# Fused local and pooled attention with a gated MLP: a new stored order, and TensorE's mask and direct pooled product kept for four head pairs instead of six

## The chip, the cores and the metric

The kernel runs on one core of one Trainium2 chip. The metric is the device time of one execution in microseconds (us). Of the kernel before, three timed runs are shown; their median is 613.86 us (613.84 to 614.27).

## The reference

Eight batches, eight heads, 576 positions, head size 64. Attention is computed twice for each head and added: once on queries, keys and values averaged over groups of 4 positions (144 of them, the result repeated 4 times), once on all positions with a mask that leaves only |i - j| < 4. The sum goes through a spatially gated MLP.

```python
q_d, k_d, v_d = (t.reshape(B, H, Sd, 4, D).mean(axis=3) for t in (q, k, v))
out_up = np.repeat(sm_attn(q_d, k_d, v_d), 4, axis=2)
scores = np.where(np.abs(pos[:, None] - pos[None, :]) < 4, scale * q @ k.T, -1e9)
x = (out_up + softmax(scores) @ v)             # heads joined: (8, 576, 512)
h = gelu_tanh(x @ w_in);  u, v = h[..., :512], h[..., 512:]
v_s = einsum('ts,bsd->btd', w_sg, layernorm(v) * g_ln) + b_sg
out = x + (u * v_s) @ w_out
```

The large products need more than one TensorE pass: each operand is split into a high and a low half, and high x high, high x low and low x high are accumulated.

## The kernel before, in words

The work is written as tasks. A task has a name, the engines it may run on and a function that emits its instructions. The string `ORDER` lists all tasks with the engine of each (`ks2/P` is task ks of pair 2 on POOL); `place` (line 60) reads it and hands out the buffers, and the loop at the end emits the tasks in that order. Each engine therefore works through its own tasks in the order of the string, and waits where an input is not there yet. Costs of tasks stand in the `add` calls, but nothing in the built program depends on them. Eight PSUM banks (`ps`), ten buffers `X` and forty buffers `R` are shared by everything. In the rows, a number behind a buffer's name is that of the tile which uses it.

There are 32 head pairs (g = 0 to 31, two heads of 64 rows beside each other), four to a batch, and one MLP block to a batch. For a pair, TensorE does:

- `S` (scores, line 408): the local scores in ten windows, 64x64 tiles, 40 instructions of line 420.
- `Y` (scores_d, 436): the pooled scores, 64x144 tiles, 12 instructions of line 442.
- `T`, `U`, `t` (turn, turn2, turn3, lines 509 to 525): transpositions of the weights of attention, 128x128 and 72x128 tiles, lines 512, 517 and 522. All three together are called turns below.
- `d` (av_d, 544): the pooled product with the values, line 552, 72x64 tiles.
- `D` (av, 565): the local product with the values, 64x58 tiles, 40 instructions of line 573.

S, Y and D contract over 64 rows; they are called 64-row work below. The MLP products are the wide work: `v` and `vk` (line 665, 128x512) and `u`, `s`, `o` (line 743, 128x288), called from `v_mm`, `u_mm`, `s_mm`, `o_mm`.

Pairs 0 to 5 are early (`early = g < EARLY`, line 365). In an early pair TensorE itself adds the mask: `scores` first writes the mask into the two banks by a product with the identity (line 413, 4 instructions), and `top` (line 451) and `exp` read the banks. In later pairs VectorE (DVE) adds the mask in two steps, `ma` and `mb` (line 428), which also free the banks, and `top` is one reduction (453). In an early pair `d` multiplies the values of all four positions of a group (32 instructions); in later pairs GpSimd (POOL) first sums them (`vs`, lines 404 and 405, four instructions) and `d` has 8 instructions.

While the first pairs run, the weights are prepared: 24 pieces of 64-bit input words are turned into a high and a low half by shift, flush, total, high and low (lines 296 to 324) on DVE, ScalarE (ACT) and POOL, and w_sg by lines near 351. The first block's `u0.x`, `s0.x` and `o0.x` need them. `gl0.3` (line 799) is the last DVE step ahead of the first output product `o0.6`.

Of the kernel before, what the change touches and what calls it, by code (L numbers as in the profile page):

```python
# [89 lines left out]
wty3/P ks4/P S3 qs4/V wby6 mx3 wqy4 wqy6 wfy4 wfy6 t1 T1 wuz5 U1 wuy6 pa1/A re2/A pb1/A d0 wby1 rc2 nx3/A Y3 why2/V  # L90
np2/V pc1/A wqy1 wty4/P why4/V wfy1 wbz4 my3 wly7/V ea3 od0 wty6/P lw2 wuz7 pe1/A T2 pa2/A nq2/P D0 wly0/P xa0
wly5/P wqz4 U2 t2 wfz4 wur2 ny3/A why6/A wuz4 ec3 wuz6 wty1/P pb2/V wly4/P d1 wbz5 pc2/V xb0 why1/V wqz5 eb3 xh0/V
why3/V wbz7 pe2/V wfz5 wly1/P wly6/P od1 wuz1 wr3 lv2 S4 wz3 lw3 lw4 wq0 wqz7 mx4 re3/A wuz0 wur1 qs5/P nx4/A ea4
eb4 lv3 lq6 wr5 wq4 wr7 lk6 wq1 xl0/P Y4 D1 my4 d2 rc3 xa1 wfz7 xb1 nq3/V wly2/V xh1/V ny4/V ec4 lv4 np3/P wbz6 wbz0
wr0 wqz6 od2 xl1/P wly3/P wqz0 re4/A S5 vk2.0 T3 wtz7/P xc1 mx5 wfz0 rc4 wfz6 vk1.0 vk2.1 D2 lw5 lq7 pa3/A t3 U3
np4/V xa2 whz7/V xb2 nx5/A ea5 vk1.1 wuz2 eb5 pb3/V pc3/V xh2/V pe3/A wtz5/P wur5 whz5/A whq3/A nq4/P vk0.0 t4 T4 U4
pa4/A wlz7/V ks5/V wtz0/P wbz1 qs6/V pb4/V whz0/A wqz1 pc4/A wuz3 d3 wbz2 wfz1 wtz4/P wtz6/P xl2/P vk0.1 wlz0/P xc2
xc0 od3 wqz2 pe4/A wbz3 whz6/A wqz3 vk1.2 wfz2 D3 xa3 wfz3 xb3 wtz1/P whz1/A xh3/A vk2.2 Y5 my5 ny5/A d4 ks6/P
wlz1/P xl3/P wbr1 ec5 wbr3 re5/V qs7/V lk7 wtz3/P wqr1 od4 wqr3 wur3 wfr1 rc5 xc3 wtz2/P wlz5/V np5/P wbr5 wfr3
# [5 lines left out]
u0.3 ua0.3 vl0.2/V Y6 T5 wbr2 wur4 wqr2 wfr7 my6 whr1/A xc4 pa5/V s0.0 sa0.0 ks8/P wtr7/P sm0.0/P wlr5/P wlr1/P ec7
ny6/A s0.1 U5 pb5/A lq8 qs8/V wbr0 wbr6 sa0.1 wqr0 ec6 whr7/V wfr2 wqr6 s0.2 sa0.2 wfr0 wtr2/V wlr7/V wfr6 pc5/V
sm0.1/P nx6/A eb6 gh0.0/A s0.3 s0.4 t5 s0.5 lv5 sm0.2/P wtr6/P sa0.3 wbr4 wtr0/P s0.6 sm0.3/P ea6 sa0.4 wqr4 re6/A
whr2/A gh0.1/A whr0/A wfr4 gl0.0/V whr6/A sa0.5 rc6 sm0.5/V sm0.4/V gl0.1/V sa0.6 pe5/A s0.7 nq6/V sa0.7 np6/V
sm0.7/V wlr2/P sm0.6/P wtr4/P wlr0/V whr4/V d5 Y8 U6 gh0.2/A my8 lw6 od5 lv6 gh0.3/A gl0.2/P D5 lw7 gl0.3/V T6 xa5
# [5 lines left out]
vg1.0 vg1.2 vb1.0 vp1.0 vb1.2 vp1.2 nq9/P va1.4/V vj1.4 T9 d8 od8 v1.1 vn1.0 pa9/V vn1.2 vg1.1 vg1.3 lv9 U9 D8 t9
vb1.1 xa8 pb9/V S10 ma10 u1.3 u1.1 u1.0 vh1.0/A ua1.2 ua1.3 vg1.4 vp1.1 vn1.1 xb8 vh1.1/A xh8/A vb1.3 lq12 os0.3
os0.1 lk11 mb10 pc9/V vp1.3 mx10 vn1.3 vh1.3/A pe9/A u1.4 Y10 ua1.0 lk12 vh1.2/A ua1.4 nx10/A ua1.1 vs9 d9 lw10
os0.2 u1.6 lv10 vb1.4 vp1.4 vl1.3/V vn1.4 od9 D9 lw11 my10 vh1.4/A vl1.1/V vl1.0/P xl8/P u1.7 ks11/P vs10 xa9 S11
vl1.4/V vl1.2/V qs12/V xb9 u1.5 ea10 ny10/A eb10 ec10 s1.4 s1.0 ma11 re10/V rc10 nq10/V xc8 np10/P ks12/P lk13 lq13
# [840 lines left out]
```

## Time and profile before

| | |
|---|---|
| median of 3 runs | 613.86 us |
| the profiled execution | 612.97 us |
| its span, first to last instruction | 611.2 us (1.8 us lie around it) |
| granted TensorE clock, mean | 0.997 |
| first TensorE instruction | 6.1 us after the span's start |
| TensorE instructions | 6600 |
| DMA | 58.10 MB, mean 95 GB/s |

The profile is of one execution. A timeline row has the start in us, the time from the first start to the last end of its instructions, the engine, the line, the operation, what it writes and reads, the tiles' shapes and the count; behind it, in brackets, the idle time ahead of it and what ended it. TensorE's instructions overlap, so what a step costs its successors is read from one start to the next start, not from the length in its row. A windows row has a stretch of the span, its length, and for PE, PEld, DVE, ACT and POOL the busy time with the number of instructions, then the granted clock, the mean busy share of the DMA engines and GB/s.

### The profile page before, as it was taken

To read this page: it belongs to the slowest core of one execution; us is meant where nothing else is said; L and a number is where in the kernel's file an instruction comes from. 1 tells how busy PE (TensorE), PEld (TensorE's weight loads), DVE (VectorE), ACT (ScalarE), POOL (GpSimd) and SP (SyncE) were. 2 spreads that over 40 slices of the span, in tenths; PEclk is the share of its full clock that TensorE was granted. 3 is DMA by queue.
4 is the path that set the end of the run, shared out by engine and by line. 5 is a ranking of instruction groups with operands and counts; after the bars stand their busy time and mean duration, and the time that the engine had idled before them with its cause. 6 is when DMAs were issued, how large, how long until landed. Compare 5 with 4: busy or idle time off the path is not lost.

```text
span 611.2 us, 16757 instructions
## 1 busy us (share of the span) xinstructions
PE 591.3 (97%) x6600; PEld 530.4 (87%) x6600; DVE 437.6 (72%) x930; ACT 335.2 (55%) x1260; POOL 323.6 (53%) x414
## 2 busy tenths in 40 slices
PE   5799999999998999999999999999999999999997
PEld 3578888988898889998899989998898888998997
DVE  5999999657786686756885677844889669744652
ACT  4998765564855358383385526545684375710300
POOL 4779677554754365623455538653586546251320
PEclk9899999999999999999999999999999999999999
DMA  8995113271020613305212520307024012000003
GB/s 299 306 303 160 56 49 116 90 228 50 35 59 6 200 60 104 102 1 172 88 44 95 163 91 15 98 5 218 22 83 143 21 40 92 32 2 20 19 1 117
DMA packets 28494, 58.10 MB, mean 95 GB/s; under 512 B 3328, under 2 KB 3584, under 8 KB 28416
## 3 DMA queue, kind: packets, MB, share of 16 engines
q1 hardware_dynamic: 28128, 56.43, 29.4%
q8 instruction: 52, 0.85, 0.6%
q10 hardware_dynamic: 288, 0.60, 0.3%
q14 instruction: 26, 0.21, 0.1%
HBM read 47.58 MB, written 9.44 MB: 93 GB/s over the span
## 4 chain that ended last, share of the span: by engine, by line
PE 83%; DVE 9%; DMA 4%; ACT 2%; POOL 1%; issue 1%; ACTq 0%; POOLq 0%
PE ps L743 48%; PE ps L665 17%; PE ps L552 4%; PE ps L573 3%; PE ps L517 3%; PE ps L420 3%; PE ps L512 2%; PE ps L442 2%; DMA R<-in_w_in_dram 2%; DMA R<-in_qT_dram 2%; DVE R L714 2%; DVE R L787 1%; ACT X L482 1%; PE ps L522 1%; DVE R L734 1%
## 5 line engine op out<-in xcount | busy, mean ns | idle before, releaser
L743 PE MATMUL ps<-wsg_h,R 128*128 128x288 f32 x576 | 122.9, 300 | 0.4 <-ACT R L490 0.4
L743 PE MATMUL ps<-R,wout_h 128*128 128x288 f32 x512 | 109.7, 301 | 2.2 <-DVE X L428 1.6
L743 PEld LDWEIGHTS ps<-wsg_h,R 128*128 128x128 f32 x576 | 93.8, 188 | 2.7 <-issue 1.0
L743 PE MATMUL ps<-wsg_l,R 128*128 128x288 f32 x320 | 92.6, 295 | 0.0
L482 ACT ACTIVATE X<-X,nb 128x64 f32<-128x64 f32 x260 | 86.8, 339 | 3.5 <-DVE nb L461 3.1
L743 PEld LDWEIGHTS ps<-R,wout_h 128*128 128x128 f32 x512 | 83.8, 188 | 5.3 <-issue 3.2
L743 PE MATMUL ps<-X,win_h 128*128 128x288 f32 x256 | 78.6, 307 | 0.1
L743 PE MATMUL ps<-X,win_l 128*128 128x288 f32 x256 | 75.7, 296 | 0.0
L743 PE MATMUL ps<-R,win_h 128*128 128x288 f32 x256 | 75.6, 295 | 0.0
L743 PE MATMUL ps<-R,wout_l 128*128 128x288 f32 x256 | 75.6, 295 | 0.0
L706 POOL TENSOR_TENSOR rs<-rs,nhalf 128x1 f32<-128x1 f32 (+1 forms) x40 | 24.6, 616 | 83.8 <-DVE rs L697 83.8
L665 PE MATMUL ps<-win_h,X 128*128 128x512 f32 x160 | 65.3, 408 | 0.0
L665 PE MATMUL ps<-win_l,X 128*128 128x512 f32 x160 | 63.1, 394 | 0.0
L743 PEld LDWEIGHTS ps<-wsg_l,R 128*128 128x128 f32 x320 | 60.3, 188 | 0.0
L592 POOL TENSOR_TENSOR R<-R,X 128x576 fp32r<-128x576 f32 x23 | 34.0, 1479 | 35.8 <-ACT X L222 21.0
L222 ACT CAST R<-R 128x512 fp32r<-128x512 f32 (+2 forms) x43 | 27.4, 640 | 44.1 <-DVE R L714 20.1
L404 POOL TENSOR_TENSOR pairs<-R 72x256 f32<-72x256 f32 x52 | 45.5, 875 | 11.3 <-DMA R<-in_v_dram 11.1
L743 PEld LDWEIGHTS ps<-X,win_h 128*128 128x128 f32 x256 | 48.2, 188 | 3.4 <-issue 1.4
L665 PE MATMUL ps<-win_h,R 128*128 128x512 f32 x128 | 50.5, 394 | 0.0
L482 ACT ACTIVATION_READ_ACCUMULATOR X<-X,nb 128x1 f32 x260 | 49.7, 191 | 0.0
L780 DVE SCALAR_TENSOR_TENSOR vs<-ps,small_sb,b_sb 128x288 f32<-128x288 f32 x64 | 32.4, 510 | 22.7 <-PE ps L743 21.5
L743 PEld LDWEIGHTS ps<-R,win_h 128*128 128x128 f32 x256 | 48.2, 188 | 0.4
(104 smaller groups left out, 1435.7 us busy)
## 6 DMA issues: line engine op xcount, KB each, us to landing
X<-in_vw_dram SPq DMA_DIRECT2D x32, 320.0 KB
R<-in_kT_dram SPq DMA_DIRECT2D x32, 293.0 KB
R<-in_v_dram SPq DMA_DIRECT2D x64, 144.0 KB
out_dram<-R SPq DMA_DIRECT2D x31, 288.0 KB
R<-in_qT_dram SPq DMA_DIRECT2D x30, 293.0 KB
R<-in_w_in_dram SPq DMA_DIRECT2D x16, 256.0 KB
R<-in_w_out_dram SPq DMA_DIRECT2D x8, 256.0 KB
R<-in_w_sgT_dram SPq DMA_DIRECT2D x5, 288.0 KB
```

Of the source, the lines that this page charges most:

```text
L222: (nc.scalar.copy if e == "A" else ENG[e].tensor_copy)(**kw)
L404: ENG[e].tensor_tensor(out=pairs, in0=v[:, 0:2], in1=v[:, 2:4], op=ALU.add)
L420: nc.tensor.matmul(out=sp[i][os, c * KB:(c + 1) * KB], lhsT=q[hs, t * QB:t * QB + KB], rhs=k[hs, t * QB:t * QB + KB], start=not early, sto ...
L482: nc.scalar.activation(out=st["ms"][:, t, :], in_=src, func=AF.Exp, bias=st["nb"][:, i * NTP + c:i * NTP + c + 1], scale=scale, accum_out= ...
L517: nc.tensor.matmul(out=out[:, i * P:(i + 1) * P], lhsT=st["pd"][:, n, keys], rhs=ident2[:, i % 2], is_transpose=True, start=True, stop=True)
L552: nc.tensor.matmul(out=dn[hs].rearrange("p (i m) -> p i m", i=3), lhsT=st["v4"][kt][:, f, hs] if early else st["vd"][:, kt, hs], rhs=pdt[: ...
L573: nc.tensor.matmul(out=at["ps", "o", g, i][hs, c * QB:(c + 1) * QB], lhsT=v[ks, c, hs], rhs=pt[ks, c, h ^ i], start=True, stop=True)
L592: ENG[e].tensor_tensor(out=r32(st["xl"]), in0=st["x"][:, 0:S], in1=st["xh"][:, 0:S], op=ALU.subtract)
L665: nc.tensor.matmul(out=acc, lhsT=r32(l), rhs=r32(w[:, k, DM:DF]), start=(i == 0 and ks[0] == 0), stop=(i == len(ops) - 1 and ks[-1] == KT ...
L706: nc.gpsimd.tensor_tensor(out=rs[0:n], in0=rs[0:n], in1=nhalf[0:n], op=ALU.pow)
L743: nc.tensor.matmul(out=acc[:, 0:HALF], lhsT=r32(l), rhs=r32(r), start=(first and n == 0), stop=(last and n == len(ops) - 1))
L780: nc.vector.scalar_tensor_tensor(out=vsb[i], in0=at["ps", "m", b, "s", i][:, 0:HALF], scalar=g_sb[:, i // 2:i // 2 + 1], in1=b_sb[:, half( ...
```

## The change

Two things change. `EARLY = 6` becomes `EARLY_S, EARLY_D = 4, 4`, so pairs 4 and 5 take the later form: mask on DVE, pooled sum of the values on POOL. And the string `ORDER` is another one, with other places and other engines for many tasks. The numbers in the `add` calls that stand for TensorE's costs change too; the program that is built does not depend on them. How far ahead the loads of a pair may run (`ahead`) stays as it was.

```diff
-EARLY = 6
+EARLY_S, EARLY_D = 4, 4
-        early = g < EARLY
+        early, early_d = g < EARLY_S, g < EARLY_D
-            parts = [(kt, f) for kt in range(2) for f in range(FAC if early else 1)]
+            parts = [(kt, f) for kt in range(2) for f in range(FAC if early_d else 1)]
-                                     lhsT=st["v4"][kt][:, f, hs] if early else st["vd"][:, kt, hs],
+                                     lhsT=st["v4"][kt][:, f, hs] if early_d else st["vd"][:, kt, hs],
-        ahead = 4 if early else 2
+        ahead = 4 if g < 6 else 2
-        if not early:
+        if not early_d:
             add(N("vs"), {"P": 2.7}, vsum, [N("lv"), N("d", 2)], gives=[("R", "v4", g, 0), ("R", "v4", g, 1)])
...
-pe10/V ny11/A ec11 ea11 sm1.0/V s1.2 sa1.2 re11/V sm1.1/V rc11 nq11/P sm1.2/P gh1.0/V d10 lv11 s1.3 od10 D10 s1.5
+pe10/V sm1.0/P ks12/P xl9/P ea11 ec11 re11/A s1.1 sa1.2 sm1.2/V rc11 d10 sa1.1 s1.3 od10 lv11 np11/V sa1.4 sm1.4/V
```

The next rows show TensorE's order at the place of pair 5's scores, behind the pooled product of pair 2. Before:

```order
L552 MATMUL ps_765<-R_634,R_659 64x144 x8
L552 MATMUL ps_765<-R_634,R_660 64x144 x8
L413 MATMUL ps_817<-small_sb 128x320
L413 MATMUL ps_818<-small_sb 128x320
L420 MATMUL ps_817<-R_295,R_374 64x64 x2
L420 MATMUL ps_818<-R_295,R_374 64x64 x2
```

And now:

```order
L552 MATMUL ps_778<-R_630,R_558 64x144 x8
L552 MATMUL ps_778<-R_630,R_559 64x144 x8
L420 MATMUL ps_807<-R_273,R_283 64x64 x2
L420 MATMUL ps_808<-R_273,R_283 64x64 x2
L420 MATMUL ps_807<-R_273,R_283 64x64 x2
```

The two instructions of line 413 that write the mask into the banks are gone; the trace before has four of them to a pair, since each is carried out in two.

The counterpart on DVE, at the top of pair 5's scores (stats_84), among the weights' steps and the merges of finished pairs. Before:

```order
L298 SCALAR_TENSOR_TENSOR ps_805<-R_301,ps_805 128x256
L451 TENSOR_REDUCE stats_84<-ps_817 128x5
L451 TENSOR_REDUCE stats_84<-ps_818 128x5
L313 SCALAR_TENSOR_TENSOR R_854<-R_301,ps_805 128x256
L501 RECIPROCAL rc_95<-sums_85 128x13
```

And now:

```order
L324 TENSOR_TENSOR win_l<-R_487,win_h 128x256
L428 TENSOR_TENSOR X_835<-ps_807,small_sb 128x5x64
L222 CAST X_837<-R_750 128x576
L428 TENSOR_TENSOR X_835<-ps_808,small_sb 128x5x64
L222 CAST win_h<-R_795 128x256
L453 TENSOR_REDUCE stats_84<-X_835 128x10
L501 RECIPROCAL rc_95<-sums_85 128x13
```

Two mask steps of line 428 have come in, and one reduction stands where two were.

TensorE again, in the second batch, between gate products (wsg): the turns T10, t10 and U10 of pair 10 with Y11, the pooled scores of pair 11 (kd_88, qd_80), among them. Before:

```order
L743 MATMUL ps_2636<-wsg_l,R_2534 128x288
L512 MATMUL ps_2670<-small_sb,X_2365 128x128 x4
L442 MATMUL ps_2675<-kd_88,qd_80 64x144 x2
L442 MATMUL ps_2676<-kd_88,qd_80 64x144 x2
L442 MATMUL ps_2675<-kd_88,qd_80 64x144 x2
L517 MATMUL ps_2683<-small_sb,R_2617 72x128 x3
L522 MATMUL ps_2689<-small_sb,X_2365 128x128
L517 MATMUL ps_2689<-small_sb,R_2617 72x128 x3
L743 MATMUL ps_2694<-wsg_h,R_2406 128x288
```

And now the same turns T10 and U10 (t10 stands elsewhere between wide products):

```order
L743 MATMUL ps_2638<-wsg_l,R_2558 128x288
L512 MATMUL ps_2658<-small_sb,X_2428 128x128 x4
L522 MATMUL ps_2664<-small_sb,X_2428 128x128
L517 MATMUL ps_2664<-small_sb,R_2525 72x128 x3
L743 MATMUL ps_2684<-wsg_h,R_2258 128x288
```

Y11 now stands three wide products earlier (u1.5, s1.0 and s1.4 lie between), directly in front of the local scores S11 of the same pair:

```order
L743 MATMUL ps_2531<-X_2114,win_l 128x288
L442 MATMUL ps_2544<-kd_88,qd_80 64x144 x2
L442 MATMUL ps_2545<-kd_88,qd_80 64x144 x2
L442 MATMUL ps_2544<-kd_88,qd_80 64x144 x2
L420 MATMUL ps_2566<-R_2089,R_2093 64x64 x2
L420 MATMUL ps_2567<-R_2089,R_2093 64x64 x2
```

A visit of 64-row work between turns is gone there, and two blocks of 64-row work that stood apart follow each other.

More of the change, by code (lines that the diff above doesn't have):

```diff
@@ L90 @@
[L90 to L99, printed above, removed]
@@ L105 @@
[L105 to L109, printed above, removed]
@@ L115 @@
[L115 to L119, printed above, removed]
@@ L160 @@
-ea23 s4.5 re23/A sm4.3/P sm4.4/V sa4.5 sm4.5/P T22 s4.7 U22 t22 pa22/A pb22/A pc22/A pe22/A rc23 gh4.1/V gl4.1/V
-gh4.2/V np23/V sa4.7 nq23/P s4.6 d22 Y24 t23 od22 sm4.7/P sa4.6 sm4.6/V gh4.3/V D22 xa22 gl4.3/V gl4.2/P T23 pa23/A
-S24 lv23 U23 o4.0 lq26 lw24 lk26 my24 ma24 xb22 pb23/A o4.3 o4.4 xh22/A mb24 vs23 xl22/P qs25/P xc22 mx24 pc23/A
-nx24/A oa4.0 pe23/V ny24/V eb24 ea24 ec24 re24/A d23 o4.5 o4.6 o4.2 od23 rc24 oa4.2 nq24/P D23 xa23 xb23 oa4.4 oa4.6
-oa4.3 ks26/V np24/P o4.1 o4.7 T24 t24 S25 xh23/A xl23/P v5.1 lv24 oa4.7 os4.3 lq27 ma25 mb25 mx25 oa4.5 oa4.1 os4.1
@@ L170 @@
-lq28 ma26 mb26 mx26 D25 Y27 ua5.5 S27 vh5.0/V nx26/A ua5.7 xa25 vl5.0/V u5.3 vs26 ma27 xb25 my27 ua5.3 xh25/A mb27
-qs28/P ny27/V ea26 eb26 re26/A s5.1 lw27 s5.0 s5.2 sa5.1 lq29 lk29 s5.5 s5.3 s5.4 qs29/P ks29/P sm5.1/P xc24 xl25/V
-xc25 mx27 sa5.0 sm5.0/V gh5.0/V sa5.2 rc26 ks28/P nx27/A ec27 np26/V eb27 sm5.2/P sa5.3 sm5.3/V T26 sa5.4 nq26/P U26
-t26 s5.6 sm5.4/V sa5.5 ea27 re27/A gh5.1/A gl5.1/P rc27 pa26/A pb26/V gl5.0/V pc26/A nq27/V sm5.5/P s5.7 np27/P
-sa5.6 pe26/V d26 sm5.6/P sa5.7 sm5.7/V gh5.3/V gl5.3/V T27 Y28 lv27 gh5.2/A od26 D26 gl5.2/P U27 pa27/A pb27/A my28
@@ new lines @@
+ks25/V gl4.0/P ea23 sm4.3/V sa4.5 gh4.1/A s4.7 sm4.5/V re23/A pa22/A rc23 nq23/P pb22/A pc22/A pe22/A sa4.4 sm4.4/V
+s4.6 sa4.7 gh4.2/A np23/V sm4.7/V sa4.6 gl4.2/P gl4.1/P d22 t23 sm4.6/V od22 Y24 D22 gh4.3/A xa22 T23 gl4.3/V S24
+pa23/A U23 lv23 lw24 o4.0 lq26 ma24 mb24 mx24 nx24/A pb23/A my24 xb22 xh22/A oa4.0 pc23/V vs23 o4.3 o4.2 o4.4 oa4.4
+qs25/V o4.6 ny24/A ea24 pe23/A d23 lk26 ec24 eb24 oa4.2 oa4.6 o4.5 od23 xl22/V re24/V rc24 D23 Y25 xc22 nq24/P
+np24/P oa4.5 xa23 oa4.3 xb23 xh23/V S25 ma25 mb25 ks26/V xl23/P o4.7 T24 o4.1 lk27 lv24 vs24 mx25 my25 u5.2 U24
@@ new lines @@
+xa25 Y27 S27 S26 xb25 ma26 my27 lk28 lq28 mb26 mx26 os4.1 lk29 lq29 vs26 u5.3 ua5.3 xh25/A xl25/P ma27 xc25 nx26/A
+ua5.7 s5.0 sa5.0 sm5.0/V s5.2 mb27 ks28/V sa5.2 ea26 eb26 s5.1 lw26 re26/A ny27/A mx27 nx27/V sa5.1 s5.4 s5.3 eb27
+ec27 ea27 re27/A sm5.2/P sm5.1/P qs29/V rc26 np26/V qs28/P nq26/P gh5.0/V sa5.3 sm5.3/V sa5.4 T26 s5.5 U26 s5.6
+pa26/A sa5.5 gh5.1/V sm5.5/V sm5.4/P rc27 t26 gl5.1/P s5.7 np27/P nq27/P gh5.2/V pb26/V pc26/A pe26/A d26 od26 lv27
+gl5.0/V sa5.6 sa5.7 sm5.6/V sm5.7/V gh5.3/V gl5.3/V T27 Y28 gl5.2/P pa27/A D26 U27 S28 ma28 xa26 pb27/A pc27/A vs27
@@ L362, in attention @@
         g = b * NPAIR + p
-        N = lambda c, back=0: f"{c}{g - back}" if g >= back and not (c == "vs" and g - back < EARLY) else None
+        N = lambda c, back=0: f"{c}{g - back}" if g >= back and not (c == "vs" and g - back < EARLY_D) else None
         par = g % 2
-        early = g < EARLY
+        early, early_d = g < EARLY_S, g < EARLY_D
         def load_q(e):
@@ L605, in attention @@
         add(N("ks"), {"V": 0.68, "P": 1.3}, ksum, [N("lk"), N("Y", 2)], gives=[("R", "k", g)])
-        if not early:
+        if not early_d:
             add(N("vs"), {"P": 2.7}, vsum, [N("lv"), N("d", 2)], gives=[("R", "v4", g, 0), ("R", "v4", g, 1)])
-        add(N("S"), {"T": 1.8 if early else 0.74}, scores, [N("lq"), N("lk"), N("D", ahead)] + (["small"] if early else []), takes=[("ps", "s", g, 0), ("ps", "s", g, 1)], gives=[("R", "q", g), ("R", "k", g)])
+        add(N("S"), {"T": 1.85 if early else 0.618}, scores, [N("lq"), N("lk"), N("D", ahead)] + (["small"] if early else []), takes=[("ps", "s", g, 0), ("ps", "s", g, 1)], gives=[("R", "q", g), ("R", "k", g)])
         if not early:
@@ L625, in attention @@
         add(N("nq"), {"P": 0.98, "V": 0.5}, norm_d, [N("rc")])
-        add(N("T"), {"T": 0.45}, turn, [N("np"), "small"], takes=[("ps", "t", g, 1)], gives=[("X", "ms", g)])
-        add(N("U"), {"T": 0.43}, turn2, [N("np"), N("nq"), "small"], takes=[("ps", "t", g, 2)], gives=[("X", "ms", g), ("R", "pd", g)])
-        add(N("t"), {"T": 0.31}, turn3, [N("nq"), "small"], takes=[("ps", "t", g, 3)], gives=[("R", "pd", g)])
+        add(N("T"), {"T": 0.454}, turn, [N("np"), "small"], takes=[("ps", "t", g, 1)], gives=[("X", "ms", g)])
+        add(N("U"), {"T": 0.461}, turn2, [N("np"), N("nq"), "small"], takes=[("ps", "t", g, 2)], gives=[("X", "ms", g), ("R", "pd", g)])
+        add(N("t"), {"T": 0.352}, turn3, [N("nq"), "small"], takes=[("ps", "t", g, 3)], gives=[("R", "pd", g)])
         add(N("pa"), {"A": 0.52, "V": 0.58}, evac(0, 4, 1), [N("T")], takes=[("R", "pt", g)], gives=[("ps", "t", g, 1)])
@@ L632, in attention @@
         add(N("pe"), {"A": 0.34, "V": 0.37}, evac_d(1, 3, 0), [N("t"), N("pc")], gives=[("ps", "t", g, 3)])
-        add(N("d"), {"T": 2.4 if early else 0.64}, av_d, [N("pc"), N("pe"), N("D", 2), N("lv" if early else "vs")], takes=[("ps", "o", g, 0)],
-            gives=[("R", "pdt", g)] + ([("R", "v4", g, 0), ("R", "v4", g, 1)] if early else []))
+        add(N("d"), {"T": 2.12 if early_d else 0.643}, av_d, [N("pc"), N("pe"), N("D", 2), N("lv" if early_d else "vs")], takes=[("ps", "o", g, 0)],
+            gives=[("R", "pdt", g)] + ([("R", "v4", g, 0), ("R", "v4", g, 1)] if early_d else []))
         add(N("od"), {"A": 0.35}, mean_d, [N("d"), N("xa", 2), N("xb", 2)])
-        add(N("D"), {"T": 0.71}, av, [N("pa"), N("pb"), N("lw"), N("d"), N("od")], takes=[("ps", "o", g, 1)],
+        add(N("D"), {"T": 0.607}, av, [N("pa"), N("pb"), N("lw"), N("d"), N("od")], takes=[("ps", "o", g, 1)],
             gives=[("R", "pt", g), ("X", "vw", g)])
@@ L823, in mlp @@
             last = s == NS - 1
-            c = 1.9 if last else 2.7
+            c = 1.9 if last else 2.8
             w = [f"wly{i}" for i in range(2 * KT)] if first else []
@@ L849, in mlp @@
             w = [f"wl{n}{j}" for n in "z" for j in range(2 * KT) if j % 2 == i // 4] if first else []
-            add(N("u", i), {"T": 1.7}, u_mm(i), xn + w, takes=[("ps", "m", b, "u", i)], gives=xs)
+            add(N("u", i), {"T": 1.651}, u_mm(i), xn + w, takes=[("ps", "m", b, "u", i)], gives=xs)
             add(N("ua", i), {"A": 0.38}, u_act(i), [N("u", i), N("ua", i - 1) if i % 2 else None], takes=[("R", "us", b, i // 2)] if i % 2 == 0 else [],
@@ L854, in mlp @@
             w = [f"wlq{s}" for s in range(NS)] + ["b", "small"] if first else []
-            add(N("s", i), {"T": 1.95}, s_mm(i), [N("vl", s) for s in range(NS)] + w,
+            add(N("s", i), {"T": 1.907}, s_mm(i), [N("vl", s) for s in range(NS)] + w,
                 takes=[("ps", "m", b, "s", i)],
@@ L869, in mlp @@
             if b == NB - 1 and i < 4:
-                add(f"ok{i}", {"T": 1.23}, o_mm(i, range(KT - 1)), [N("gl", d) for d in range(KT - 1)], takes=take)
+                add(f"ok{i}", {"T": 1.22}, o_mm(i, range(KT - 1)), [N("gl", d) for d in range(KT - 1)], takes=take)
                 take, ks = [], range(KT - 1, KT)
                 w = [f"ok{i}"]
-            add(N("o", i), {"T": 1.66 * len(ks) / KT}, o_mm(i, ks), [N("gl", d) for d in range(KT)] + w, takes=take,
+            add(N("o", i), {"T": 1.62 * len(ks) / KT}, o_mm(i, ks), [N("gl", d) for d in range(KT)] + w, takes=take,
                 gives=[("R", c, b, d) for c in ("gh", "gl") for d in range(KT)])
```

182 lines of the change are left out of this document (101 added, 81 removed).

## The prediction

> **What bounds the kernel now.** I read the page first, then the busy times of three stretches, then TensorE's timeline at single places.
>
> ```profile
> PE 591.3 (97%) x6600; PEld 530.4 (87%) x6600; DVE 437.6 (72%) x930; ACT 335.2 (55%) x1260; POOL 323.6 (53%) x414
> ```
>
> ```profile
> 10.00:106.50 96.50, 89.06 (x1207) 74.33 (x1199) 90.66 (x216) 78.09 (x321) 73.17 (x90) 0.98 0.58 176
> 106.50:611.20 504.70, 498.30 (x5378) 453.80 (x5378) 344.04 (x709) 255.74 (x940) 248.14 (x315) 1.00 0.24 76
> ...
> 40.00:50.00 10.00, 10.00 (x144) 8.01 (x141) 9.93 (x25) 9.36 (x54) 8.75 (x10) 1.00 1.04 300
> ```
>
> TensorE is busy for 97% of the span, so an average says "TensorE". The stretches say more. Up to 106.5 us DVE is busy for 90.66 of 96.5 us, in the third row for 9.93 of 10, with ACT and POOL close behind; I call this stretch A. After it DVE is busy for 344 of 505 us and TensorE for 498: stretch B is TensorE's alone. The cut is the start of o0.6, the first output product, which waits for DVE:
>
> ```profile
> 106.47 0.40 PE L743 MATMUL ps<-R,wout_h 128*128 128x288 f32 x1 [0.53 <-DVE R L580]
> ```
>
> **What a change of form costs TensorE.** Busy time hides the prices, because the next instruction's start is what a step delays. First local scores S11 alone between wide products; then the chain D25, Y27, S27; then turns between wide products (the last row is v1.2's first product); then a stretch in which turns and 64-row work alternate (Y24, t23, D22, T23, S24, U23).
>
> ```profile
> 157.67 0.30 PE L743 MATMUL ps<-R,win_h 128*128 128x288 f32 x1
> 157.81 0.29 PE L743 MATMUL ps<-X,win_l 128*128 128x288 f32 x1
> 158.03 0.81 PE L420 MATMUL ps<-R,R 64*64 64x64 f32 x40
> 158.77 0.40 PE L743 MATMUL ps<-X,win_h 128*128 128x288 f32 x1
> 159.01 0.29 PE L743 MATMUL ps<-R,win_h 128*128 128x288 f32 x1
> ...
> 444.86 0.81 PE L573 MATMUL ps<-R,X 64*64 64x58 f32 x40
> 445.49 0.56 PE L442 MATMUL ps<-kd,qd 64*64 64x144 f32 x10
> 446.68 0.40 PE L743 MATMUL ps<-X,win_h 128*128 128x288 f32 x1
> ...
> 126.32 0.49 PE L517 MATMUL ps<-small_sb,R 128*72 128x128 f32 x3
> 126.65 0.60 PE L512 MATMUL ps<-small_sb,X 128*128 128x128 f32 x4
> 127.08 0.27 PE L522 MATMUL ps<-small_sb,X 128*128 128x128 f32 x1
> 127.44 0.48 PE L665 MATMUL ps<-win_h,X 128*128 128x512 f32 x1
> ...
> 394.16 0.71 PE L442 MATMUL ps<-kd,qd 64*64 64x144 f32 x12
> 394.80 0.52 PE L517 MATMUL ps<-small_sb,R 128*72 128x128 f32 x3
> 395.25 0.81 PE L573 MATMUL ps<-R,X 64*64 64x58 f32 x40
> 395.99 0.66 PE L512 MATMUL ps<-small_sb,X 128*128 128x128 f32 x4
> 396.57 0.81 PE L420 MATMUL ps<-R,R 64*64 64x64 f32 x40
> 397.32 0.33 PE L522 MATMUL ps<-small_sb,X 128*128 128x128 f32 x1
> 397.48 0.49 PE L517 MATMUL ps<-small_sb,R 128*72 128x128 f32 x3
> 397.73 0.38 PE L743 MATMUL ps<-R,wout_h 128*128 128x288 f32 x1
> 397.95 0.29 PE L743 MATMUL ps<-R,wout_l 128*128 128x288 f32 x1
> ```
>
> From start to start: a wide product takes 0.14 us (157.67 to 157.81), but 0.22 when 64-row work follows and 0.24 when it comes first after 64-row work (158.77 to 159.01). So each visit of 64-row work costs 0.09 ahead of it and 0.11 behind it. Alone, S takes 0.74, Y 0.64 (394.16 to 394.80) and D 0.74 (395.25 to 395.99), together 2.12; as a chain they take 1.82 (444.86 to 446.68), 0.30 less for two joints: 0.15 to a joint. A turn depends on what follows. T takes 0.43 ahead of another turn (126.65 to 127.08) and 0.58 ahead of 64-row work (395.99 to 396.57). U takes 0.36 ahead of a wide product (127.08 to 127.44), and I give T the same. t takes 0.33 ahead of a turn, 0.45 ahead of 64-row work (394.80 to 395.25) and 0.25 ahead of a wide product (three such instructions from 397.48 to 397.73). The first wide product behind a turn takes 0.22 (397.73 to 397.95), 0.09 above its pace.
>
> [...]
>
> **Stretch B, term by term.** I counted in both orders what follows what on TensorE from o0.6 on. The number of blocks is the same: 73 of 64-row work, 50 T and U, 26 t, 26 d.
> - *Turns.* T and U stand ahead of a wide product 24 times before and 39 now, ahead of a turn 17 and 5, ahead of 64-row work or d 9 and 6: 24 x 0.36 + 17 x 0.43 + 9 x 0.58 = 21.2 us against 39 x 0.36 + 5 x 0.43 + 6 x 0.58 = 19.7. For t it is 9, 10 and 7 against 22, 2 and 2: 8.7 against 7.1. Together -3.1 us.
> - *64-row work.* The 73 blocks stand in 56 visits before and 39 now, so 17 joints are gained: 17 x 0.15 = -2.5 us.
> - *Borders of wide products.* 64-row work follows a wide product 39 times before and 28 now, and precedes one 41 and 27 times; a turn precedes one 33 and 61 times. -11 x 0.09 - 14 x 0.11 + 28 x 0.09 = 0.0 us.
>
> B's TensorE time falls by 5.6 us. It lies on the path: nothing else is as full there. If no price is carried by the change of form itself but only by the place, the term is 0; that end stays for the range.
>
> **Stretch A, term by term.** Pair 4's mask and scores (36.18 to 38.09) and pair 2's direct product d2 (39.39 to 41.50) stand here beside a later pair's d (214.66 to 215.30).
>
> ```profile
> 36.18 1.34 PE L413 MATMUL ps<-small_sb 128*128 128x320 f32 x4
> 37.46 0.81 PE L420 MATMUL ps<-R,R 64*64 64x64 f32 x40
> 38.09 0.54 PE L442 MATMUL ps<-kd,qd 64*64 64x144 f32 x10
> ...
> 39.39 2.18 PE L552 MATMUL ps<-R,R 72*64 72x144 f32 x32
> 41.50 1.34 PE L413 MATMUL ps<-small_sb 128*128 128x320 f32 x4
> ...
> 214.66 0.71 PE L552 MATMUL ps<-R,vd 72*64 72x144 f32 x8
> 215.30 0.40 PE L743 MATMUL ps<-R,wout_h 128*128 128x288 f32 x1
> ```
>
> S falls from 1.91 to 0.74 and d from 2.11 to 0.64, for two pairs 2 x (1.17 + 1.47) = 5.3 us of TensorE. How much of that becomes time is set by DVE. The change gives DVE two masks a pair, and POOL two pooled sums:
>
> ```profile
> L428 DVE TENSOR_TENSOR X<-ps,small_sb 128x320 f32<-128x320 f32 x52 | 24.1, 481 | 3.2 <-PE ps L420 3.0
> L404 POOL TENSOR_TENSOR pairs<-R 72x256 f32<-72x256 f32 x52 | 45.5, 875 | 11.3 <-DMA R<-in_v_dram 11.1
> L405 POOL TENSOR_TENSOR vd<-pairs 72x128 f32<-72x128 f32 x52 | 28.4, 546 | 4.1
> ```
>
> The masks are 4 x 0.48 = 1.9 us on DVE. But the new order also hands steps from one engine to another: up to gl0.3, behind which o0.6 starts, DVE has 219 instructions before and 212 now, the masks among them. At the stretch's mean of 90.66 / 216 = 0.42 us that is 2.9 us less. DVE's idle time in A is 5.8 us. So the bounds are: none of TensorE's gain, if the steps that left DVE were short ones and its idle time stays; all 5.3 us, if DVE's own work falls by 2.9 and 2.4 of its 5.8 idle us go, which an earlier TensorE might do.
>
> Against DVE stands POOL: two pooled sums a pair are 2 x (0.875 + 0.546) = 2.8 us, 5.7 us for two pairs, and POOL slows DVE. The same gate step on DVE takes 0.96 us beside a running POOL step and 0.45 without:
>
> ```profile
> 315.79 0.91 POOL L507 TENSOR_TENSOR R<-R,rc 128x432 f32<-128x432 f32 x1 [3.55 <-DVE vs L780]
> 316.06 0.96 DVE L787 TENSOR_TENSOR R<-R,vs 128x288 f32<-128x288 f32 x1
> 317.68 0.45 DVE L787 TENSOR_TENSOR R<-R,vs 128x288 f32<-128x288 f32 x1
> ```
>
> At worst 5.7 us of POOL work cost DVE half of that, 2.9 us. [...]
>
> I take A at -2.9 + 0.5 = -2.4 us, between 0 and -5.3.
>
> **The sum.** -5.6 - 2.4 = -8.0 us, with TensorE's waits in B as long as they are. Against the profiled execution's 612.97 that is 605.0; the median of the runs is 0.9 higher, 613.86, so I forecast 605.9. Start and end, 6.1 us ahead of the first product and the last store, keep their steps.
>
> **Rivals.**
> - *TensorE sets A too.* DVE's order is so much better that all 5.3 us arrive: -10.9, 603.0. For it: 7 DVE instructions fewer. Against: 9.93 of 10 us busy. Chance 0.12.
> - *Held at both ends.* A brings nothing and new waits eat half of B: -2.8, 611.1. For it: engines behind TensorE get 8 us less time for the same work. Chance 0.16.
> - *The prices do not move.* What I read as the price of a change of form belongs to the place, and the new order pays it elsewhere: B is 0, A -2.4, 611.5. Against: S alone between wide products shows it in three rows. Chance 0.10.
> - *Slower: joints that wait.* A chain of D, Y and S needs its inputs and up to five banks at once, and the product behind it may take a bank that the mask has not left. That stands in the trace once already, at o1.4 behind S13:
>
> ```profile
> PE ps L743 <- DVE X L428: 1.6, 1, 1.6
> ```
>
>  Each of the 17 new joints can cost such 1.6 us. Five eat the gain; at six (9.6 us) it is slower, and seven give -8.0 + 11.2 = +3.2, 617.1. Against: between a pair's scores and its turns the new order leaves at least 9.2 us of TensorE work at the prices above, before it was 8.5, so inputs are as far ahead as they were. Chance 0.06.
>
> **How the numbers follow.** The forecast has the remaining 0.56, its own range 603.2 to 609.0 (A between 0 and -5.3, B's waits 2 us either way, not both at their ends). The range 602.2 to 611.2 leaves out the slower rival, and part of the ends of the others. A measurement of this kernel can tell about 0.2%, 1.2 us, from no change: faster is below 612.6. The forecast, the first rival and most of the second and third lie there, 0.90; same 0.05, from the edges of these two; slower 0.05.
>
> **What would show it.** TensorE 6544 instructions instead of 6600, line 413 x16, line 552 with vd x224; o0.6 about 2.4 us earlier, near 104; from o0.6 to the end about 5.6 us less; T and U at 0.36 and t at 0.25 in most places. DVE still over nine tenths busy up to o0.6. I am wrong if o0.6 starts later than 106.5 us, if B's part is shorter by less than 3 us, or if TensorE shows waits of over 1 us at more than three places in B.

## The result, and the profile after

The changed kernel takes 602.82 us (median of 4 runs, 602.69 to 603.04) against 613.88 for the kernel before (median of 4 runs): ratio 0.9819, 95% interval 0.9802 to 0.9836, 11.06 us less. Beside the kernels of the experiments the kernel before took 614.0 to 614.5 us in the median with single runs from 612.4 to 619.2, the longer ones at a lower mean granted clock (617.44 us at 0.986, 613.75 at 0.997). The changed kernel's profiled execution took 602.69 us, its span is 600.9. First the page's busy times of the changed kernel, then the busy times of the two stretches and of ten microseconds in the first.

```profile
PE 578.5 (96%) x6544; PEld 524.9 (87%) x6544; DVE 435.2 (72%) x925; ACT 336.2 (56%) x1270; POOL 324.2 (54%) x417
```

```profile
10.00:103.40 93.40, 82.97 (x1152) 69.36 (x1150) 88.44 (x203) 78.22 (x319) 75.35 (x94) 1.00 0.53 172
103.40:600.90 497.50, 492.41 (x5378) 453.59 (x5378) 342.37 (x713) 254.64 (x945) 246.44 (x315) 1.00 0.26 79
...
40.00:50.00 10.00, 9.14 (x156) 7.40 (x148) 9.97 (x22) 9.02 (x49) 7.79 (x10) 1.00 0.86 274
```

The columns are the window, its length, the busy time of PE, PEld, DVE, ACT and POOL, the granted clock, the DMA share and GB/s. DVE is still busy for 88.44 of 93.4 us ahead of o0.6, and TensorE for 492 of 497.5 behind it. The cut itself, on TensorE's timeline of the changed kernel, S7 and then the first product of o0.6:

```profile
102.53 0.81 PE L420 MATMUL ps<-R,R 64*64 64x64 f32 x40
103.42 0.40 PE L743 MATMUL ps<-R,wout_h 128*128 128x288 f32 x1
```

o0.6 starts at 103.42 instead of 106.47: stretch A gave 3.06 us. From there to the start of TensorE's last block, o7.7, it is 492.65 us instead of 499.84: stretch B gave 7.19. The wait for DVE that the row of o0.6 had (0.53 us) is gone. It was for pair 5's merge (line 580), which frees a bank and in the kernel before follows gl0.3 on DVE:

```profile
105.13 0.92 DVE L799 TENSOR_TENSOR R<-R,R 128x576 fp32r<-128x576 f32 x1
105.97 0.45 DVE L580 TENSOR_TENSOR R<-ps,od 128x290 f32<-128x290 f32 x1
```

In the new order that merge stands behind o0.6 and starts at 106.11. gl0.3 itself doesn't hold o0.6's start: it is the second of these two and ends at 104.54, when o0.6 has been running for 1.1 us, and only the last of o0.6's twelve products reads it.

```profile
102.06 2.48 DVE L799 TENSOR_TENSOR R<-R,R 128x576 fp32r<-128x576 f32 x2
```

The groups show the change of kinds: line 413 has 16 instructions instead of 24, and two pairs of the direct pooled product have moved from the row with R,R to the one with vd.

```profile
L552 PE MATMUL ps<-R,vd 72*64 72x144 f32 x224 | 19.9, 299 | 0.0
L552 PE MATMUL ps<-R,R 72*64 72x144 f32 x128 | 8.7, 289 | 0.5 <-DVE R L222 0.3 <-DVE R L313 0.3
L413 PE MATMUL ps<-small_sb 128*128 128x320 f32 x16 | 6.9, 562 | 4.7 <-ACT R L490 2.1 <-ACT X L482 2.0 <-DMA small_sb<-in_small_dram 0.6
```

TensorE's waits in stretch B, as the view of waits has them (total, times, longest), of the kernel before and of the changed one:

```profile
PE ps L743 <- DVE X L428: 1.6, 1, 1.6
PE ps L552 <- DVE R L222: 1.0, 1, 1.0
PE ps L512 <- POOL X L504: 0.5, 1, 0.5
```

```profile
PE ps L743 <- DVE R L580: 1.0, 1, 1.0
PE ps L420 <- DVE R L580: 0.7, 1, 0.7
PE ps L743 <- DVE X L428: 0.3, 1, 0.3
```

Other products wait now, 2.0 us in all instead of 3.1.

**Where B's 7.19 us came from.** I added up TensorE's time from the start of each block to the start of the next, by kind, in both traces:

```
stretch B            before    after   difference   forecast
turns T, U, t         30.23    26.90      -3.33       -3.1
64-row S, Y, D        49.40    49.00      -0.40       -2.5
wide products        402.34   400.08      -2.26        0.0
d                     17.86    16.67      -1.19        none
```

The turns came as forecast: T and U 21.63 to 19.87 us, t 8.60 to 7.03; 33 of 50 T and U now take 0.36 (within 0.03), 21 of 26 t take 0.25. The 64-row work holds two new waits, 1.08 us at S23 and 0.91 at S14 (their times above the pace of their kind); without them it fell by 2.4. The wide products lost two waits, 1.75 at o1.4 and 0.74 at s1.0, and gained one of 0.41 at o5.3; without them they fell by 0.2. What d lost is one wait of 1.2 at d26. So the prices gave -3.3 - 2.4 - 0.2 = -5.9, and the waits, 3.7 before and 2.4 after, gave -1.3.

### The profile page after: what moved, and what is told of

Same layout as the page of the kernel before. It is cut to its first block, busy times and chain, and to the rows that moved or that the text cites. A ratio compares the mean times of both kernels' runs of the same rounds, so it can differ in the third digit from the quotient of the medians.

```text
span 600.9 us, 16628 instructions
## 1 busy us (share of the span) xinstructions
PE 578.5 (96%) x6544; PEld 524.9 (87%) x6544; DVE 435.2 (72%) x925; ACT 336.2 (56%) x1270; POOL 324.2 (54%) x417
## 4 chain that ended last, share of the span: by engine, by line
PE 79%; DVE 10%; DMA 4%; ACT 4%; issue 1%; POOL 1%; SPq 0%; DVEq 0%; ACTq 0%; POOLq 0%
PE ps L743 49%; PE ps L665 15%; PE ps L552 3%; PE ps L573 3%; PE ps L517 3%; PE ps L420 2%; DMA R<-in_w_in_dram 2%; PE ps L512 2%; PE ps L442 2%; ACT X L482 1%; DMA R<-in_qT_dram 1%; DVE R L222 1%; DMA X<-in_vw_dram 1%; DVE R L787 1%; DVE st L695 1%
## 5 line engine op out<-in xcount | busy, mean ns | idle before, releaser
L743 PE MATMUL ps<-R,wout_h 128*128 128x288 f32 x512 | 111.2, 302 | 0.4 <-DVE X L428 0.3
L482 ACT ACTIVATE X<-X,nb 128x64 f32<-128x64 f32 x280 | 93.5, 338 | 13.0 <-DVE nb L461 12.6
L222 ACT COPY R<-ps 72x288 f32<-72x288 f32 (+2 forms) x87 | 32.7, 408 | 42.3 <-PE ps L517 14.9
L482 ACT ACTIVATION_READ_ACCUMULATOR X<-X,nb 128x1 f32 x280 | 53.4, 191 | 0.0
L222 ACT CAST R<-R 128x576 fp32r<-128x576 f32 (+2 forms) x35 | 22.6, 646 | 49.0 <-DVE R L714 21.0
L743 PEld LDWEIGHTS ps<-R,wout_l 128*128 128x128 f32 x256 | 48.2, 188 | 0.0
```

Of the source, the lines that this page charges most:

```text
L222: (nc.scalar.copy if e == "A" else ENG[e].tensor_copy)(**kw)
L482: nc.scalar.activation(out=st["ms"][:, t, :], in_=src, func=AF.Exp, bias=st["nb"][:, i * NTP + c:i * NTP + c + 1], scale=scale, accum_out= ...
L743: nc.tensor.matmul(out=acc[:, 0:HALF], lhsT=r32(l), rhs=r32(r), start=(first and n == 0), stop=(last and n == len(ops) - 1))
```

## The experiments

Theory of the forecast: prices of form set stretch B, DVE sets stretch A. Rivals: the prices belong to the place; TensorE sets A too; moved blocks wait. Single runs of one kernel spread too far for differences of 1 or 2 us, so these are read from the traces, by the start of o0.6 and by B's length from there to the start of o7.7. Five traces with the changed kernel's stretch A untouched have o0.6 at 103.42, 103.47, 103.55, 103.64 and 103.74 us: 0.3 us is what repeats differ by. (In the last four the granted clock was 0.83 from 20 to 30 us, in the first, the changed kernel's own, 1.00.) Ratios are to runs of the kernel before taken beside each kernel's. In some of these kernels the line numbers are one higher.

```
                                  us      ratio to before, 95%      o0.6        B
before                          613.88                             106.47    499.84
changed                         602.82    0.9802 to 0.9836         103.42    492.65
both kinds for six pairs        609.06    0.9861 to 0.9929         108.11    493.10
mask for six                    604.52    0.9788 to 0.9854         105.26    492.48
pooled product for six          606.45    0.9819 to 0.9894         106.23    493.15
old order, kinds for four       616.80    0.9990 to 1.0039         108.63    501.48
DVE masks twice, in A           604.98    0.9800 to 0.9864         104.91    492.65
DVE masks twice, in B           604.26    0.9791 to 0.9855         103.64    493.60
D twice, in A                   605.05    0.9801 to 0.9871         105.76    492.63
D twice, in B                   604.90    0.9804 to 0.9871         103.74    494.58
before, six Y joined            623.74    1.0111 to 1.0164         106.47    509.57
changed, 15 Y taken out         607.56    0.9858 to 0.9905         103.55    497.27
before, two waits moved         612.00    0.9936 to 0.9991         111.06    497.70
changed, two waits moved        602.62    0.9777 to 0.9831         103.47    491.86
```

**Stretch A: the kinds undone in the new order.** Three kernels put pairs 4 and 5 back, both kinds and each alone:

```diff
-    EARLY_S, EARLY_D = 4, 4
+    EARLY_S, EARLY_D = 6, 6
...
-... ma4 mb4 ... ma5 mb5 ... vs4 ... vs5 ...
```

With the mask go ma and mb of the two pairs, with the pooled product vs4 and vs5; the first two kernels also hand on ea5 and eb5 in the other order, wbz0 behind ea4 and vk1.0 behind ea5. Expected, for both, for the mask, for the pooled product:

> The changed kernel with pairs 4 and 5 put back to the old way: TensorE's mask and the direct pooled product for six pairs; the two DVE masks and POOL's pooled sums of these pairs are gone, and three steps move a few places because banks are held longer. TensorE's own work up to o0.6 is 5.5 us more by the rows, DVE's 1.9 us less, POOL's 2.8 less. If DVE sets stretch A (the forecast's reason): at or a little under the changed kernel's 602.8, between -2 and +1.5 us, o0.6 at 102 to 105 us, DVE still over nine tenths busy. If TensorE sets A (the rival): +4.5 to +5.5 us, about 608, o0.6 near 108.5. Stretch B is within 0.5 us of the changed kernel's 492.7 under both.

> The changed kernel with TensorE's mask for six pairs again, the direct pooled product for four. TensorE +2.6 us up to o0.6, DVE -1.9 us (four masks). DVE sets A: -1.9 to +0.5 us. TensorE sets A: +2.0 to +2.6 us, about 605.2. Together with the next run it parts the two halves of the change of kinds.

> The changed kernel with the direct pooled product for six pairs again, TensorE's mask for four. TensorE +2.9 us up to o0.6, POOL -2.8 us, DVE nothing of its own. If DVE sets A and POOL costs it as the forecast took it: -0.5 to +0.5 us. If TensorE sets A: +2.5 to +2.9 us, about 605.5. If POOL's pressure on DVE is the upper bound of the forecast: -1.5 us.

Measured: o0.6 comes 4.4 to 4.7 us later with both, 1.5 to 1.8 with the mask, 2.5 to 2.8 with the pooled product. That is the rival's answer; the mask alone stays under the 2.0 to 2.6 us that the rival had for it. The granted clock doesn't explain it: from 20 to 30 us it was 0.83, 1.00 and 0.67 in the three kernels, and S4, behind that, starts within 0.16 us of the changed kernel's. Where the time enters is seen from the starts of single blocks on TensorE, each against the changed kernel's (us):

```
                      S4     d1     D2     t4     d3     D4     Y8    o0.6
changed, start      35.1   36.3   44.1   47.9   51.3   60.9  100.7   103.4
both for six       -0.02  +1.15  +3.27  +3.41  +1.97  +3.44  +4.84   +4.70
mask for six       -0.16  +1.01  +3.15  +3.29  +1.84  +1.85  +1.84   +1.84
pooled for six     +0.13  +0.13  +0.23  +0.21  +0.12  +1.57  +2.96   +2.81
DVE masks twice    -0.04  -0.04  +0.99  +1.77  +1.35  +1.35  +1.50   +1.50
D twice            +0.12  +0.12  +0.72  +2.36  +1.19  +1.77  +2.32   +2.34
```

From d3 on, at 51 us, almost nothing is absorbed: d4 and d5 as direct products cost 1.45 and 1.47 us (the pooled run, from d3 to D4 and across d5), where the forecast's rows have 1.47, and all but 0.15 of it arrives at o0.6. Ahead of d3 part is absorbed: U4, right behind t4, waits 0.86 us for DVE anyway, and 1.4 us of what the masks brought is gone behind it. The view of waits says the same of the changed kernel, from 51 us to the cut:

```profile
PE ps L442 <- ACT R L761: 0.8, 1, 0.8
PE ps L743 <- POOL R L734: 0.7, 1, 0.7
PE ps L552 <- DVE R L222: 0.3, 1, 0.3
```

TensorE waits for 1.8 us in these 52. It sets the second half of A, while DVE is nearly as full beside it. The busy times of the halves of the changed kernel:

```profile
10.00:51.00 41.00, 32.34 (x588) 24.43 (x586) 38.73 (x99) 38.11 (x199) 32.86 (x44) 1.00 0.96 318
51.00:104.00 53.00, 51.22 (x569) 45.51 (x569) 50.32 (x105) 40.22 (x120) 43.09 (x52) 1.00 0.20 61
```

In the first half TensorE has 8.7 us of idle time and DVE 2.3; in the second TensorE has 1.8.

**The charge for POOL.** The windows up to the cut of the kernel with both kinds for six and of the one with the mask alone for six; they differ by two pairs' pooled sums on POOL and have the same 212 DVE steps.

```profile
0.00:10.00 10.00, 3.02 (x16) 1.94 (x16) 4.35 (x11) 3.26 (x8) 2.37 (x10) 1.00 0.83 265
10.00:108.10 98.10, 89.05 (x1208) 74.80 (x1206) 86.84 (x201) 77.77 (x319) 72.27 (x88) 0.98 0.52 166
```

```profile
0.00:10.00 10.00, 3.17 (x16) 1.94 (x16) 4.49 (x12) 3.43 (x10) 2.51 (x10) 1.00 0.81 266
10.00:105.30 95.30, 85.16 (x1161) 70.94 (x1159) 86.50 (x200) 77.72 (x319) 75.45 (x94) 1.00 0.52 169
```

DVE is busy for 4.35 + 86.84 = 91.19 us without the sums and for 4.49 + 86.50 = 90.99 with them. They cost DVE nothing here. A longer DVE step beside POOL is not refuted by that: the forecast's two rows show it at line 787, 0.96 us beside a POOL step and 0.45 without, and in the trace of the kernel before the 44 steps of that line on DVE take 0.43 to 1.66 us. The 52 masks of line 428 take 0.47 to 0.49 us there, with a POOL step beside them or without. These sums fell beside steps that ran at the length they have in the kernel before too: in the kernel with the sums, the reductions of line 388 (0.74 us) and steps that read or write PSUM (lines 297, 299, 314 and 781 there, 0.41 to 0.51 us); only the end of the second sum met a gate product (788).

**The kinds in the old order.** The kernel before with EARLY_S and EARLY_D at 4; the masks stand behind S4 and S5, vs4 behind xl2 and vs5 behind sm0.3:

```diff
-... S4 ...
+... S4 ma4 mb4 ...
-... xl2 ...
+... xl2 vs4 ...
```

> The old order with only the kinds changed: pairs 4 and 5 lose TensorE's mask and the direct pooled product, their masks stand right behind their scores on DVE, their pooled sums on POOL as late as they can. TensorE up to o0.6 is 5.45 us less by the rows, DVE 1.9 us more. If DVE sets A: 0 to +2 us against the kernel before (613.9 to 616), so that all of the change's gain in A is the order's. If TensorE sets A: -4 to -5.4 us, about 609. The forecast's -2.4 for A needed DVE's 7 fewer instructions, which this run doesn't have. Stretch B as in the kernel before, 499.8, within 0.5 us.

Measured: 616.80 us, and o0.6 at 108.63, 2.2 us later than before, with 5.45 us less of TensorE work. That is the answer of "DVE sets A". The freed time turned into waits. The longest is at o0.6 itself, for the same merge of pair 5 that held it for 0.53 us in the kernel before, with DVE busy all the while:

```profile
100.00:106.00 6.00, 5.14 (x110) 4.09 (x112) 6.00 (x9) 2.12 (x4) 4.51 (x5) 1.00 0.57 182
```

```profile
108.63 0.48 PE L744 MATMUL ps<-R,wout_h 128*128 128x288 f32 x1 [2.29 <-DVE R L581]
```

One that the view of waits didn't have in the kernel before is a product of v (line 666) that waits for POOL's low part of x:

```profile
PE ps L666 <- POOL R L593: 1.4, 1, 1.4
```

Behind each of these two waits the granted clock is 0.50:

```profile
61.10:64.30 3.20, 3.20 (x46) 2.19 (x44) 3.10 (x10) 3.19 (x6) 3.12 (x6) 0.50 0.03 5
108.90:112.10 3.20, 3.20 (x15) 3.20 (x15) 2.02 (x5) 1.81 (x11) 1.57 (x3) 0.50 0.67 260
```

How much of the 2.2 us the first of these makes wasn't parted. The second is B's excess: B is 1.6 us longer than before, 1.2 of it in o0.6, whose products start every 0.24 us instead of 0.13.

So in A the change is a pair of halves of which neither helps alone: the new order with six pairs is 1.6 us slower than before (108.11 against 106.47), the kinds in the old order gain nothing (2.2 slower, in part by the clock), both together are 3.1 faster. Another placement of the new steps in the old order might do better; only this one was run.

**Work added to one engine.** The changed kernel with DVE's masks of three pairs done twice, or with D of four pairs done twice, in A and in B; each repeat writes the same values again.

```diff
+                for _ in range(2 if g in (4, 5, 6) else 1):
...
-            for c in range(NTP):
+            for c in [c for _ in range(2 if g in (1, 2, 3, 4) else 1) for c in range(NTP)]:
```

> The changed kernel with DVE's masks of pairs 4, 5 and 6 done twice with the same result, six additions of 0.48 us, 2.9 us of DVE in stretch A. If DVE sets A: +2 to +2.9 us, about 605.3. If TensorE sets A: 0 to +0.7 us.

> The same doubled masks for pairs 10, 19 and 28 in stretch B, 2.9 us of DVE. DVE is seven tenths busy there: 0 to +0.5 us under both theories. It is the control of the doubled masks in A.

> The changed kernel with the local value products (D) of pairs 1 to 4 done twice with the same result, four times 0.6 to 0.74 us, 2.4 to 3.0 us of TensorE in stretch A. If DVE sets A: 0 to +1 us. If TensorE sets A: +2.4 to +3.0 us, about 605.5.

> The same doubled D for pairs 10, 15, 20 and 25 in stretch B, 2.4 to 3.0 us of TensorE, all of it time under both theories: +2.4 to +3.0 us. It is the control, and gives the price of a D behind a D.

The four D cost 1.9 us in B (0.48 for a D behind a D, less than the 0.6 expected) and 2.0 to 2.3 in A: all of TensorE's added time arrives in A as well. The six masks, 2.9 us of DVE, cost 1.2 to 1.5 in A. The table above shows which: those of pairs 4 and 5, ahead of 51 us, cost 1.35; those of pair 6, behind it, 0.15. In B they cost 0.9 instead of at most 0.5: 0.6 of it comes between o5.3 and o5.5, beside pair 28's masks, 0.3 near o3.2. Here a full DVE cost time at the places where a product waited for it, not by its busy share.

**The prices of form.** Six Y joined to other 64-row work in the old order, and 15 Y taken out of their chains in the new one. One word of each:

```diff
-... Y19 ... my19 ... D17 ...
+... Y19 my19 D17 ...
...
-... S19 ... Y20 ... s3.3 ... s3.2 ...
+... S19 ... s3.3 ... Y20 ... s3.2 ...
```

> The kernel before with six pooled scores of stretch B (Y10, Y14, Y18, Y19, Y24, Y25) moved by two to eight places on TensorE so that each stands beside an S, D or Y; nothing else moves but my19, behind its Y. If the prices of the form are real: six joints at 0.15 us and the borders saved, -1.5 us by the rows (-2.1 if every border of 0.2 goes), 612.4 to 611.8. If the price belongs to the place: 0, within 0.5 us.

> The changed kernel with 15 pooled scores of stretch B taken out of their chain of 64-row work and put between two wide products, at most five places away on TensorE. If the prices of the form are real: 15 x 0.40 = +6.1 us by the rows, about 608.9, with TensorE's waits in B as they are (2.6 us), or longer where a Y came later. If the price belongs to the place: 0 to +1 us.

Taken out: B is 4.6 us longer, 497.27 against 492.65, where the rows said 6.1 and the place said 0 to 1. Waits ran the other way: the view of waits has 1.3 us of them left in B instead of 2.0. Eight of the 15 with no wait beside them cost 0.31 to 0.38 us each from the traces, not the 0.40 of the rows; 15 at 0.34 are 5.1, less 0.7 for the waits 4.4, near the 4.6. Y20 in that kernel between wide products, and in the changed kernel behind S19:

```profile
305.32 0.71 PE L443 MATMUL ps<-kd,qd 64*64 64x144 f32 x12
305.95 0.53 PE L744 MATMUL ps<-wsg_h,R 128*128 128x288 f32 x2
```

```profile
301.82 0.70 PE L420 MATMUL ps<-R,R 64*64 64x64 f32 x36
302.34 0.66 PE L442 MATMUL ps<-kd,qd 64*64 64x144 f32 x12
302.93 0.53 PE L743 MATMUL ps<-wsg_h,R 128*128 128x288 f32 x2
```

From Y's start to the next product's it is 0.63 us alone and 0.59 in the chain; what the chain saves besides lies at Y's other border and in S19, whose last product Y's first overlaps.

Joined: 623.74 us, 9.7 us of B more, where either theory said less or nothing. Four of the six joints did what the rows say: the start of the next wide block behind the joint moves by -0.15 (Y10), -0.33 (Y14), -0.16 (Y19) and -0.16 us (Y24), -0.8 together. The other two wait. Y18, moved up to S18, waits for a bank that line 762's activation holds, and puts 2.4 us on the path; Y25, moved eight places down, comes so late that what hangs on it is late too, 7.9 us in three steps, of which the view names two:

```profile
PE ps L443 <- ACT R L491: 2.6, 1, 2.6
PE ps L666 <- DVE R L683: 2.6, 1, 2.6
```

The third, 2.7 us, is v5.0 with the turn and the border behind it: after the two waits the granted clock is 0.50 (437.1 to 443.7 us), and v5.0's products start every 0.43 us, while the same products start every 0.23 at the full clock (v5.3, just ahead).

```profile
438.52 0.63 PE L666 MATMUL ps<-win_l,X 128*128 128x512 f32 x1
438.95 0.63 PE L666 MATMUL ps<-win_h,R 128*128 128x512 f32 x1
```

That is the forecast's slower rival as a mechanism: a joint was worth 0.15 to 0.35 us and cost 2.4 and 7.9 us at these two places. It doesn't occur in the changed kernel; there the steps around the joints were moved too, but that this is the reason was not tried.

**Waits in B.** DVE steps moved ahead of others, two in the kernel before (first cut) and three in the changed kernel (second cut):

```diff
-... Y12 S13 my12 ny12/V mb12 ...
+... Y12 S13 mb12 my12 ny12/V ...
-... nq27/V sm5.5/P s5.7 np27/P sa5.6 pe26/V d26 ...
+... pe26/V nq27/V sm5.5/P s5.7 np27/P sa5.6 d26 ...
```

```diff
-... mx22 ... xa21 ...
+... xa21 mx22 ...
-... vn2.4 xa12 xb12 ...
+... xa12 xb12 vn2.4 ...
```

> The kernel before with two DVE steps moved ahead, for the two longest waits of TensorE in stretch B: the second mask of pair 12 ahead of the maximum of its pooled scores (o1.6 waits 1.6 us for its bank), and pair 26's last evacuation ahead of pair 27's pooled normalisation (d26 waits 1.2 us). If waits in B are time on the path: -2.4 to -2.8 us, 611.1 to 611.5. If the next late thing stands right behind: under -0.5 us.

> The changed kernel with three DVE steps moved ahead, for the two longest waits that TensorE has left in stretch B: pair 21's first merge ahead of pair 22's maximum (u4.4 waits 1.0 us for its bank), and pair 12's two merges ahead of the normalisation vn2.4 (S14 waits 0.9 us for its bank). If these waits are time on the path: -1.6 to -2.0 us against the changed kernel's 602.8, and stretch B at 490.7 to 491.1 us instead of 492.7. If the next late thing stands right behind: under -0.5 us, B over 492.2. Stretch A is as in the changed kernel, o0.6 at 103.4 to 103.8.

In the kernel before, both waits went (1.75 and 1.2 us less at o1.6 and behind d26), 0.6 came back at o5.3, and B is 2.1 us shorter. The view of waits of that kernel in B:

```profile
PE ps L513 <- POOL X L505: 0.5, 1, 0.5
PE ps L744 <- DVE R L223: 0.4, 1, 0.4
```

In the changed kernel S14's wait went (0.94), and of u4.4's 1.08 only the place changed, 0.71 came back at the next block, s4.0, and 0.46 ahead of o4.0; B is 0.8 us shorter:

```profile
PE ps L744 <- DVE R L581: 0.5, 1, 0.5
PE ps L744 <- DVE X L429: 0.3, 1, 0.3
```

Its 602.62 us stand beside runs of the kernel before at 614.54, ratio 0.9804; against the changed kernel's 0.9819 the intervals overlap, so that it is faster than the changed kernel is seen in the trace's B alone.

## Why the prediction was right, and where it was not

The forecast was 605.9, faster; it is 602.8, within the range of 602.2 to 611.2 and 0.4 below the forecast's own 603.2 to 609.0. Step by step:

- **B's prices: held.** -5.6 forecast, -5.9 measured, and each term of it within 0.2 us. The rival that the prices don't move with the form fails at 15 Y taken out (+4.6) and at the four joints without a wait (-0.8).
- **B's waits: the term that was mis-sized.** "TensorE's waits in B as long as they are" was a 0 with 2 us either way; it measured -1.3. The two kernels with moved DVE steps show that such waits are time on the path, 2.1 of 2.9 us in the one and 0.8 of 2.0 in the other. The order removed some for good. A smaller part of the difference is not of the kernels: the forecast carried over the 0.9 us between the profiled execution before (612.97) and the median; for the changed kernel that is 0.1.
- **A's size: nearly held, by luck. A's reason: fell.** -2.4 forecast, -3.06 measured. But "How much of that becomes time is set by DVE" failed for the changed kernel. DVE's 7 fewer instructions were to bring 2.9 us; its busy time up to the cut fell from 2.88 + 90.66 = 93.54 to 4.42 + 88.44 = 92.86, by 0.7. What happened instead: TensorE sets A from 51 us on, and the kinds give 4.4 to 4.7 of their 5.3 us in the new order; the new order itself takes 1.6 back. It starts later (S2 at 16.7 us instead of 14.8, d1 at 36.3 instead of 34.1), the shorter S4 and S5 make that good (d4 at 56.6 and 56.4), and d4 and d5 as pooled products give their 2 x 1.47 = 2.9 behind it. For the old order the sentence holds, as far as one placement shows: there o0.6 waits for a DVE step, 0.53 us before and 2.29 with the kinds alone, and TensorE's 5.45 us bring nothing. The new order puts that step behind o0.6. I read "9.93 of 10 us busy" as a bound, in a row in which TensorE had 10.00 of 10.
- **POOL's charge of 0.5: not there.** No run shows the 0.5; DVE's work is the same with and without two pairs' pooled sums on POOL (90.99 and 91.19 us). Of the bound of 2.9, which carried the one step of 0.96 us instead of 0.45 over to all of POOL's time, nothing is seen there either.
- **The rival "TensorE sets A too"** was right in its mechanism, for the second half. Its 603.0 is close to the result, but by another sum: it had 5.3 from A, which gave 3.1, and nothing from the waits in B.
- **The slower rival** needed six waits of 1.6 us; the changed kernel has one over 1 us in B. Joints moved by hand in the old order show that it is real, at two places of six.

Of what was to show it, TensorE's 6544 instructions, lines 413 and 552, the start of o0.6 near 104, the turns' times and DVE's busy share all came as said; the last was true and decided nothing. From o0.6 to the end it was 7.2 us less instead of 5.6.

## What to carry to other kernels

Two engines at nine tenths in the same stretch say nothing of which one sets its end: look at where each of them waits, and add a known piece of work to one of them at two places. Where an order was searched for one set of work, neither the order nor the work can be judged without the other; here the order alone lost 1.6 us, the work alone gained nothing, and both together gained 3.1. A block moved beside its like on TensorE saved 0.15 to 0.35 us here, and where the steps that free its bank or its successors' stayed behind, TensorE waited.
